# A decode step's output projection and second MLP layer: weights as the moving operand in four column strips, and the output in four transfers

## The chip, the cores and the metric

The kernel runs on one core of a Trainium2 chip. The metric is the device time of one execution in microseconds (us). The five engines run their own instruction streams and signal one another through semaphores: PE (TensorE; its weight loads are listed apart as PEld), DVE (VectorE), ACT (ScalarE), POOL (GpSimd) and SP (SyncE). SP and ACT also issue transfers (DMA).

## The reference

A decode step for 4 sequences, one token each, in bf16. An attention branch over the last 1024 positions of the caches (32 query heads, 8 key/value heads) and an MLP branch share a normalised input; the MLP's result gates the attention's.

```python
# x: (4, 1, 512); caches (4, 8, 4096, 128); wq (512, 4096); wo (4096, 512)
# w1 (512, 1792), b1 (1792); w2 (1792, 512), b2 (512)
xn = layernorm(x)
q = xn @ wq                                   # 32 heads of 128
k, v = caches[:, :, Sk - 1024:, :], each repeated for 4 heads
p = softmax(q @ k.T * 128 ** -0.5)
s = (p @ v).reshape(4, 1, 4096) @ wo          # output projection
h = gelu(layernorm(xn) @ w1 + b1)
g = silu(h @ w2 + b2)                         # second MLP layer
out = x + s * g                               # (4, 1, 512)
```

## The kernel before, in words

All input comes through SP's queue in one written-out order: `wq`, the eight key groups (one per key/value head, 1 MB each), then value group 0, `w1`, value group 1, `w2`, value groups 2 to 7, and `wo` in six pieces (three of 1 MB, then 512, 384 and 128 KB). Value group g takes the buffer of key group g and waits until that group has been transposed. ACT's queue carries the small inputs: x (L184), `b1` (L185), `b2` (L187) and, after the first norm's square root, x once more (`x16`, L251) as 16 rows of 128 for the end.

A small scheduler (`_Program`) keeps one list of operations per engine, in the order in which the program adds them. Before an operation it waits on the semaphores of those it names; every transfer has a semaphore of its own that rises by 16. Nothing is reordered: what is added first on an engine runs first there.

POOL makes the constants (identity, selection matrices, masks; also `ident32`, an identity in f32). DVE and ACT compute the two norms. PE then works through 32 tiles of keys: transpose (L278), copy by DVE (L284), scores (L297). The q projection (L362) uses four column strips: a `tile_position=(0, 32*s)` gives 32 of the array's columns to output partitions 32s to 32s+31. For each of the 8 groups, `PV` multiplies the exponentials with the values (L315) and sums the exponentials (L321), and `epilogue` divides on DVE (L328 to L333).

The MLP lies between the groups. `mlp1` (L400, L404) comes after group 0; `mlp2` and `mlp3` after group 1; `mlp4` after group 2's PV. `mlp3` first puts the bias into PSUM (L435) and then adds 14 x 4 matmuls (L442), each with a 128x128 block of `w2` as the stationary operand and 4 columns of `hT`, one per sequence, as the moving one. The result `psM[:, PS_Z:...]` has feature p of block c in partition p, column c*4+b. ACT takes the tanh (L447), and DVE makes the gate `g_sb` (L451, L453).

After the last group `to_rows` (L486, L493) collects the attention output into `OW`, 4 columns per group and quarter. `wo` then adds 128 matmuls (L507), six batches that each wait for one piece of the weight, in the same form as L442: a 128x128 block of `wo_sb` stationary, 4 columns of `OW` moving. The end is a chain: DVE multiplies with the gate (L534, 128x16), PE transposes to 16 rows of 128 (L538, in f32), DVE adds `x16` (L540), SP issues the output (L542) and waits for it.

```python
    v = add("dve", lambda e: e.tensor_tensor(
        bass.AP(sg_sb, 0, [[16, 128], [1, 4], [4, 4]]),
        psM[:, PS_W:PS_W + 16].rearrange("p (c b) -> p c b", c=4),
        g_sb[:, :].rearrange("p (c b) -> p c b", c=4), ALU.mult), t_w, mlp["g"])
    t = add("pe", lambda pe: pe.transpose(psS[0][0:16, 0:128], sg_sb[:, :], ident32[:, :]),
            v, c_id32, ex[HKV - 2])
    v = add("dve", lambda e: e.tensor_tensor(o_bf[:, :], psS[0][0:16, 0:128], x16[:, :], ALU.add),
            t, *d_x16)
    d_out = pg.dma("sp", "out", lambda e: e.dma_start(
        out.rearrange("b s (c p) -> (b s c) p", p=128), o_bf[:, :]), v)
```

Of the kernel before, what the change touches and what calls it, by code (L numbers as in the profile page):

```python
# [16 lines left out]
class _Program:  # L17
# [10 lines left out]
    def add(self, eng, fn, *deps):  # L28
        op = _Op(eng, fn, deps)
        self.ops[eng].append(op)  # L30
        return op
# [42 lines left out]
def bass_recurrent_scan__sliding_block_cached__mixer_channel_mlp__decode_kernel(  # L74
# [14 lines left out]
    ALU = mybir.AluOpType  # L89
    AF = mybir.ActivationFunctionType  # L90
    AX = mybir.AxisListType
    BF16 = dt.bfloat16
    F32 = dt.float32

    B, D = 4, 512
    HQ, HKV, DH = 32, 8, 128
# [4 lines left out]
    FC = F // 128  # L101
# [14 lines left out]
    sb = nc.alloc_sbuf_tensor  # L116
# [7 lines left out]
    w2_sb = sb([128, FC, D], BF16)  # L124
# [1 line left out]
    P_buf = sb([128, HKV, NC * 16], BF16)  # L126

    x_bf = sb([4, 512], BF16)
    x16 = sb([16, 128], BF16)

    x32 = P_buf[0:4, 4:6, :].rearrange("p g n -> p (g n)").bitcast(F32)
    xn32 = P_buf[0:4, 6:8, :].rearrange("p g n -> p (g n)").bitcast(F32)
# [12 lines left out]

    ones_bf = sb([128, 128], BF16)
    ident = sb([128, 128], BF16)
    ones32 = sb([128, 128], F32)
    ident32 = sb([128, 128], F32)
    ind = sb([128, 128], BF16)  # L150
    zero_bf = sb([128, 512], BF16)
    negm = sb([128, 512], BF16)
# [3 lines left out]
    q_sb = sb([128, 2, 512], BF16)  # L156
    qT = sb([128, 128], BF16)
    b1_sb = sb([1, F], BF16)
    b2_sb = sb([4, 128], BF16)
    sel = sb([128, 4, 32], BF16)  # L160
    OW = sb([128, 4, HKV * 4], BF16)
    hT = sb([128, 64], BF16)
# [2 lines left out]
    den_sb = sb([128, HKV * 16], F32)  # L165
    rden = sb([128, HKV * 16], F32)

    tz_sb = sb([128, 16], F32)
    sz_sb = sb([128, 16], F32)
    g_sb = sb([128, 16], F32)  # L170
    sg_sb = sb([128, 16], F32)
    o_bf = sb([16, 128], BF16)

    psK = [nc.alloc_psum_tensor("psK%d" % i, [128, 1024], BF16) for i in range(NB)]
    psS = [nc.alloc_psum_tensor("psS%d" % i, [128, 512], F32) for i in range(2)]
    psO = [nc.alloc_psum_tensor("psO%d" % i, [128, 512], F32) for i in range(2)]
    psM = nc.alloc_psum_tensor("psM", [128, 512], F32)
    PS_Z, PS_W = 192, 208

    pg = _Program(nc)  # L180
    add = pg.add
# [3 lines left out]
    d_b1 = pg.dma("act", "b1", lambda e: e.dma_start(  # L185
        b1_sb[0:1, :], B_b1.rearrange("(o n) -> o n", o=1)))
    d_b2 = pg.dma("act", "b2", lambda e: e.dma_start(  # L187
        b2_sb[:, :], B_b2.rearrange("(c n) -> c n", c=4)))

    def cache_rows(cache, g):  # L190

# [7 lines left out]
    def load_k(g):  # L199
        d_k[g] = pg.dma("sp", "k%d" % g, lambda e: e.dma_start(  # L200
            kv_buf[:, g, :, :].rearrange("p c d -> p (c d)"), cache_rows(A_k_cache, g)),
            )
# [15 lines left out]
    d_wq.append(load_wq(1))  # L218
    for g in range(2, HKV):
        load_k(g)  # L220
    x_r = A_x.rearrange("b s (c p) -> (b s c) p", p=128)


    c_1 = add("gp", lambda e: e.memset(ones_bf[:, :], 1.0))
    c_id = add("gp", lambda e: e.affine_select(
        ident[:, :], ones_bf[:, :], [[1, 128]], ALU.is_equal, 0.0,
        base=0, channel_multiplier=-1), c_1)
    c_ind = add("gp", lambda e: e.affine_select(
        ind[:, :], ones_bf[:, :], [[0, 32], [1, 4]], ALU.is_equal, 0.0,
        base=0, channel_multiplier=-1), c_1)  # L230
    c_sel = add("gp", lambda e: e.affine_select(
        sel[:, :, :], ones_bf[:, :], [[1, 4], [4, 32]], ALU.is_equal, 0.0,
        base=0, channel_multiplier=-1), c_1)
    c_xT = add("gp", lambda e: e.memset(xT[:, :, :], 0.0))
    c_yT = add("gp", lambda e: e.memset(yT[:, :, :], 0.0))
    c_z = add("gp", lambda e: e.memset(zero_bf[:, :], 0.0))
    c_neg = add("gp", lambda e: e.affine_select(
        negm[:, :], zero_bf[:, :], [[0, 32], [1, 4], [0, 4]], ALU.is_equal, NEG,
        base=0, channel_multiplier=-1), c_z)
    c_o32 = add("gp", lambda e: e.memset(ones32[:, :], 1.0))  # L240
    c_id32 = add("gp", lambda e: e.affine_select(
        ident32[:, :], ones32[:, :], [[1, 128]], ALU.is_equal, 0.0,
        base=0, channel_multiplier=-1), c_o32)


    v = add("dve", lambda e: e.tensor_copy(x32[:, :], x_bf[:, :]), d_x)  # L246
    v = add("dve", lambda e: e.bn_stats(st1[:, :], x32[:, :]), v)
    v = add("dve", lambda e: e.bn_aggr(mv1[:, :], st1[:, :]), v)
    v = add("dve", lambda e: e.tensor_single_scalar(vt1[:, :], mv1[:, 1:2], EPS, ALU.add), v)
    a = add("act", lambda e: e.activation(sq1[:, :], vt1[:, :], AF.Sqrt), v)  # L250
    d_x16 = [pg.dma("act", "x16%d" % i, lambda e, i=i: e.dma_start(  # L251
        x16[8 * i:8 * i + 8, :], x_r[8 * i:8 * i + 8, :])) for i in range(2)]
    v = add("dve", lambda e: e.reciprocal(rstd1[:, :], sq1[:, :]), a)
    v = add("dve", lambda e: e.tensor_scalar(xn32[:, :], x32[:, :], mv1[:, 0:1], rstd1[:, 0:1],
                                             op0=ALU.subtract, op1=ALU.mult), v)
    v_xn = add("dve", lambda e: e.tensor_copy(xn_bf[:, :], xn32[:, :]), v)
    v = add("dve", lambda e: e.bn_stats(st2[:, :], xn32[:, :]), v)
    v = add("dve", lambda e: e.bn_aggr(mv2[:, :], st2[:, :]), v)
    v = add("dve", lambda e: e.tensor_single_scalar(vt2[:, :], mv2[:, 1:2], EPS, ALU.add), v)
    a = add("act", lambda e: e.activation(sq2[:, :], vt2[:, :], AF.Sqrt), v)  # L260
    v = add("dve", lambda e: e.reciprocal(rstd2[:, :], sq2[:, :]), a)
# [6 lines left out]
    ex = [None] * HKV  # L268
# [118 lines left out]
    mlp = {}  # L387
# [44 lines left out]

    def mlp3():
        def fn(pe):
            last = pe.matmul(psM[:, PS_Z:PS_Z + 16], b2_sb[:, :],  # L435
                             bass.AP(ident, 0, [[128, 4], [1, 4], [0, 4]]),
                             start=True, stop=False, skip_group_check=True)
            for k in range(FC):
                s = min(k // 4, 2) if k < FC - 4 else 3
                n = (k - K0[s]) * 16 + s * 4  # L440
                for c in range(4):
                    last = pe.matmul(psM[:, PS_Z + c * 4:PS_Z + (c + 1) * 4],  # L442
                                     w2_sb[:, k, c * 128:(c + 1) * 128], hT[:, n:n + 4],
                                     start=False, stop=(k == FC - 1), skip_group_check=True)
            return last
        t = add("pe", fn, mlp["h"], d_w2, d_b2, c_id)
        mlp["tz"] = add("act", lambda e: e.activation(  # L447
            tz_sb[:, :], psM[:, PS_Z:PS_Z + 16], AF.Tanh, scale=0.5), t)

    def mlp4():  # L450
        v = add("dve", lambda e: e.tensor_scalar(sz_sb[:, :], tz_sb[:, :], 0.5, 0.5,  # L451
                                                 op0=ALU.mult, op1=ALU.add), mlp["tz"])
        mlp["g"] = add("dve", lambda e: e.tensor_tensor(  # L453
            g_sb[:, :], psM[:, PS_Z:PS_Z + 16], sz_sb[:, :], ALU.mult), v)

    NUN = HKV * NU
    for n in range(LAG, NUN + LAG):
# [7 lines left out]
    d_w2 = pg.dma("sp", "w2", lambda e: e.dma_start(  # L465
        w2_sb[:, :, :], B_w2.rearrange("(p c) o -> p c o", c=FC)))
# [30 lines left out]
    first = [True]  # L497

    def wo(k, rows):
        g0, g1, i0, i1, d = d_wo[k]  # L500

        def fn(pe):
            last = None
            for g in range(g0, g1):
                for i in range(i0, i1):
                    for c in range(4):
                        last = pe.matmul(psM[:, PS_W + c * 4:PS_W + (c + 1) * 4],  # L507
                                         wo_sb[:, g, i, c * 128:(c + 1) * 128],
                                         OW[:, i, g * 4:(g + 1) * 4],
                                         start=first[0], stop=(k == len(d_wo) - 1 and i == i1 - 1),  # L510
                                         skip_group_check=True)
                        first[0] = False
            return last
        return add("pe", fn, d, rows, mlp["g"])

    for g in range(HKV):
        PV(g)
        if g == 0:
            epilogue(0)
            mlp1()  # L520
        if g >= 2:
            epilogue(g - 1)
        if g == 1:
            mlp2()
            mlp3()
        if g == 2:
            mlp4()
    epilogue(HKV - 1)
    rows = to_rows(0, HKV)
    for k in range(len(d_wo)):  # L530
        t_w = wo(k, rows)


    v = add("dve", lambda e: e.tensor_tensor(  # L534
        bass.AP(sg_sb, 0, [[16, 128], [1, 4], [4, 4]]),
        psM[:, PS_W:PS_W + 16].rearrange("p (c b) -> p c b", c=4),
        g_sb[:, :].rearrange("p (c b) -> p c b", c=4), ALU.mult), t_w, mlp["g"])
    t = add("pe", lambda pe: pe.transpose(psS[0][0:16, 0:128], sg_sb[:, :], ident32[:, :]),  # L538
            v, c_id32, ex[HKV - 2])
    v = add("dve", lambda e: e.tensor_tensor(o_bf[:, :], psS[0][0:16, 0:128], x16[:, :], ALU.add),  # L540
            t, *d_x16)
    d_out = pg.dma("sp", "out", lambda e: e.dma_start(  # L542
        out.rearrange("b s (c p) -> (b s c) p", p=128), o_bf[:, :]), v)

    pg.plan()
    with nc.Block() as block:

        @block.gpsimd
        def _(gp):
            pg.emit("gp", gp)  # L550

        @block.vector
        def _(dve):
            pg.emit("dve", dve)

        @block.scalar
        def _(act):
            pg.emit("act", act)

        @block.sync  # L560
        def _(sp):
            pg.emit("sp", sp)
            sp.wait_ge(d_out.sem, 16)

        @block.tensor
        def _(pe):
            pg.emit("pe", pe)
# [28 lines left out]
```

The softmax here doesn't subtract the row's maximum and nothing guards it: scores larger than these inputs give would overflow.

## Time and profile before

| | |
|---|---|
| median of 12 runs | 77.04 us (76.89 to 77.14) |
| the profiled execution's own time | 77.06 us |
| its span, first to last instruction | 75.3 us |
| moved by DMA | 28.99 MB, mean 385 GB/s |
| PE busy | 51.5 us (68%), 1058 matmuls |
| DVE busy | 39.3 us (52%) |
| ACT busy | 9.8 us (13%) |
| mean granted TensorE clock | 0.826 of full speed |

How to read it: times count from the span's start. The page cuts the span into 40 slices; a digit is a busy share or a granted clock in tenths, 9 standing for 90% or more. A row of the groups gives the line, the engine, the operation, out<-in with partitions x elements, the count, then the total busy us and the mean ns of one, then the idle time just before and what ended it. In a row such as `128*32` the first number is the rows of the array that are used and the second its columns. "issue" is time in which an engine waited for nothing that the profile shows. Matmuls are pipelined: their mean length is not their spacing.

### The profile page before, as it was taken

What the parts mean: (1) busy time and instruction counts of PE and PEld (TensorE: products, weight loads), DVE (VectorE), ACT (ScalarE), POOL (GpSimd) and SP (SyncE); (2) the same over time, 40 slices, a digit from 0 to 9 for tenths busy, and PEclk for the clock granted to TensorE, in tenths of its full rate; (3) what the DMA queues carried; (4) which work ended last, traced back from release to release, by engine and by line L of the source; (5) the groups of instructions that cost most, each with busy time, mean ns of one, the idle gap of its engine ahead of it and who ended that gap; (6) DMA issues with size and microseconds to landing.
All of it is one profiled execution on the core that took longest, in us unless ns stands there. A gap on an engine that the chain in (4) does not pass through costs nothing.

```text
span 75.3 us, 2309 instructions
## 1 busy us (share of the span) xinstructions
PE 51.5 (68%) x1058; PEld 39.4 (52%) x1058; DVE 39.3 (52%) x82; ACT 9.8 (13%) x16; POOL 4.6 (6%) x14
## 2 busy tenths in 40 slices
PE   0000039974789999979959987994399999365850
PEld 0000039963269989969949911022198668164730
DVE  0878106894258989969957060004654877810010
ACT  0611000000270320303303500015000000000000
POOL 6980000000000000000000000000000000000000
PEclk9999999999999999999999996599555555555555
DMA  2899999998999999999999999999999999999600
GB/s 46 270 420 405 429 431 461 452 418 378 435 422 426 422 422 431 413 435 460 412 405 439 433 420 411 422 413 422 435 426 426 424 400 420 420 418 410 255 8 2
DMA packets 4219, 28.99 MB, mean 385 GB/s; under 512 B 493, under 2 KB 625, under 8 KB 1650
## 3 DMA queue, kind: packets, MB, share of 16 engines
q1 hardware_dynamic: 4160, 28.84, 92.1%
q8 instruction: 8, 0.13, 0.6%
q10 hardware_dynamic: 50, 0.01, 0.1%
q14 instruction: 1, 0.01, 0.0%
HBM read 28.85 MB, written 0.00 MB: 383 GB/s over the span
## 4 chain that ended last, share of the span: by engine, by line
DMA 37%; PE 34%; SPq 17%; DVE 5%; issue 4%
DMA wo_sb<-in_A_wo_dram 24%; PE psK L278 21%; SPq L475 16%; DMA kv_buf<-in_A_k_cache_dram 12%; PE psS L297 6%; DVE kt_buf L284 3%; PE psO L362 3%; PE psS L293 2%; DVE q_sb L368 1%; PE psK L374 1%; PE psM L507 1%; PE psK L346 1%; PE psS L538 1%; SPq L212 1%; SPq L205 0%
## 5 line engine op out<-in xcount | busy, mean ns | idle before, releaser
L278 PE MATMUL psK<-ident,kv_buf 128*128 128x128 bf16 x256 | 20.7, 233 | 12.2 <-DMA kv_buf<-in_A_k_cache_dram 10.7
L284 DVE COPY kt_buf<-psK 128x1024 bf16<-128x1024 bf16 x32 | 21.2, 691 | 7.9 <-PE psK L278 7.7
L278 PEld LDWEIGHTS psK<-ident,kv_buf 128*128 128x128 bf16 x256 | 16.6, 105 | 11.8 <-DMA kv_buf<-in_A_k_cache_dram 10.7
L297 PE MATMUL psS<-qT,kt_buf 128*128 128x16 bf16 x256 | 10.4, 169 | 0.2 <-issue 0.2
L297 PEld LDWEIGHTS psS<-qT,kt_buf 128*128 128x128 bf16 x256 | 9.4, 96 | 1.8 <-issue 0.9
L315 PEld LDWEIGHTS psO<-P_buf,kv_buf 128*128 128x128 bf16 x256 | 7.4, 102 | 3.0 <-issue 3.0
L315 PE MATMUL psO<-P_buf,kv_buf 128*128 128x16 bf16 x256 | 8.0, 173 | 0.2
L328 DVE TENSOR_REDUCE den_sb<-psS 128x16 f32<-128x512 f32 x8 | 5.5, 691 | 4.2 <-PE psS L321 3.9
L305 ACT ACTIVATE P_buf<-psS 128x512 bf16<-128x512 f32 x8 | 4.8, 597 | 16.5 <-PE psS L297 16.5
L507 PE MATMUL psM<-OW,wo_sb 128*128 128x4 bf16 x128 | 4.2, 166 | 2.1 <-DMA wo_sb<-in_A_wo_dram 1.0
L400 PE MATMUL psK<-w_sb,yT 128*32 128x512 bf16 x16 | 4.9, 1084 | 0.8 <-issue 0.8
L507 PEld LDWEIGHTS psM<-OW,wo_sb 128*128 128x128 bf16 x128 | 3.8, 104 | 2.5 <-issue 1.2
L321 PE MATMUL psS<-P_buf,ones_bf 128*128 128x512 bf16 x8 | 4.3, 534 | 0.0
L411 DVE SCALAR_TENSOR_TENSOR kt_buf<-kt_buf,psK 128x512 f32<-128x512 f32 x1 | 0.7, 689 | 6.1 <-ACT kt_buf L410 6.1
L534 DVE TENSOR_TENSOR sg_sb<-psM,g_sb 128x16 f32<-128x16 f32 x1 | 0.2, 185 | 5.9 <-PE psM L507 5.9
L293 PE MATMUL psS<-negm,ind 128*128 128x512 bf16 x8 | 3.0, 380 | 0.0
L400 PEld LDWEIGHTS psK<-w_sb,yT 128*32 128x32 bf16 x16 | 0.5, 114 | 3.6 <-issue 3.6
L369 ACT ACTIVATE q_sb<-psO 128x512 bf16<-128x512 f32 x1 | 0.6, 597 | 13.3 <-PE psO L362 13.3
L331 DVE RECIPROCAL rden<-den_sb 128x16 f32<-128x16 f32 x8 | 2.0, 253 | 0.3
L246 DVE CAST P_buf<-x_bf 4x512 f32<-4x512 bf16 x1 | 1.0, 953 | 2.2 <-DMA x_bf<-in_A_x_dram 2.2
L362 PE MATMUL psO<-wq_sb,xT 128*32 128x512 bf16 x32 | 1.9, 380 | 0.3 <-DVE xT L351 0.3
L424 PE MATMUL psK<-ident,kt_buf 128*128 128x128 bf16 x4 | 0.6, 305 | 2.1 <-DVE kt_buf L419 2.1
(64 smaller groups left out, 28.8 us busy)
## 6 DMA issues: line engine op xcount, KB each, us to landing
kv_buf<-in_A_k_cache_dram SPq DMA_DIRECT2D x8, 1024.0 KB, 20.6
kv_buf<-in_A_v_cache_dram SPq DMA_DIRECT2D x8, 1024.0 KB, 23.8
wq_sb<-in_A_wq_dram SPq DMA_DIRECT2D x2, 2048.0 KB, 11.4
w_sb<-in_B_w_dram SPq DMA_DIRECT2D x2, 1792.0 KB, 28.0
wo_sb<-in_A_wo_dram SPq DMA_DIRECT2D x3, 1024.0 KB, 25.0
wo_sb<-in_A_wo_dram SPq DMA_DIRECT2D x1, 512.0 KB, 21.6
wo_sb<-in_A_wo_dram SPq DMA_DIRECT2D x1, 384.0 KB, 18.3
wo_sb<-in_A_wo_dram SPq DMA_DIRECT2D x1, 128.0 KB, 18.1
```

Source lines behind the costliest of these rows:

```text
L278: last = pe.transpose(psK[n % NB][:, j * 128:(j + 1) * 128], kv_buf[:, g, u * UT + j, :], ident[:, :])
L284: cp[n] = add("dve", lambda e: e.tensor_copy(kt_buf[:, n % NKT, :], psK[n % NB][:, 0:1024]), t, sc.get(n - NKT))
L293: pe.matmul(psS[g % 2][:, 0:512], ind[:, :], negm[:, :], start=True, stop=False, skip_group_check=True)
L297: last = pe.matmul(psS[g % 2][:, c * 16:(c + 1) * 16], kt_buf[:, n % NKT, j * 128:(j + 1) * 128], qT[:, g * 16:(g + 1) * 16], start=False, ...
L305: ex[g] = add("act", lambda e: e.activation(P_buf[:, g, :], psS[g % 2][:, 0:512], AF.Exp, scale=SCALE), sc[n])
L315: last = pe.matmul(pso[:, 0:16], kv_buf[:, (HKV + g) % NS, c, :], P_buf[:, g, c * 16:(c + 1) * 16], start=(c == 0), stop=(c == NC - 1))
L321: den[g] = add("pe", lambda pe: pe.matmul(psS[g % 2][:, 0:512], ones_bf[:, :], P_buf[:, g, :], start=True, stop=True), ex[HKV - 2 + g % 2] ...
L328: v = add("dve", lambda e: e.tensor_reduce(den_sb[:, cs], bass.AP(psS[g % 2], 0, [[512, 128], [1, 16], [16, NC]]), AX.X, ALU.add), den[g])
L362: last = pe.matmul(psO[m // 4][32 * s:32 * s + 32, 0:512], xT[:, c, :], wq_sb[:, c, m * 512:(m + 1) * 512], start=(c == 0), stop=(c == 3), ...
L400: pe.matmul(psK[0][32 * s:32 * s + 32, 0:1024].bitcast(F32), yT[:, c, :], bass.AP(w1_sb, c * F + K0[s], [[4 * F, 128], [1, 4], [FC, 128]]) ...
L475: e.dma_start(wo_sb[:, g0:g1, i0:i1, :], wo_r[:, g0:g1, i0:i1, :]))))
L507: last = pe.matmul(psM[:, PS_W + c * 4:PS_W + (c + 1) * 4], wo_sb[:, g, i, c * 128:(c + 1) * 128], OW[:, i, g * 4:(g + 1) * 4], start=firs ...
```

## The change

Both operands of L442 and L507 change places. The 4 columns of `hT` or `OW` become the stationary operand, loaded into one of four column strips, and 128 columns of the weights become the moving one. Block c of the output features goes to strip c: sequence b is partition 32c+b, and its 128 features lie along the row. The first matmul of each strip loads 32 columns instead of 4, so that all 128 partitions of the PSUM area are written. The bias is added last, by four matmuls with one row of ones.

The tanh, the gate, the product and the sum now work on 128x128 instead of 128x16. The result has its features along the rows already, so the transpose, `ident32` and `ones32` go. x comes as `xs`, 4 rows into the start of each strip, by four transfers on ACT's queue that wait for a memset of `xs`; the output leaves by four transfers of 4 rows, two on SP's queue and two on ACT's. `b2` is loaded as one row. The numbers of instructions and the order on each engine are otherwise as they were.

```diff
-    x16 = sb([16, 128], BF16)
+    xs = sb([128, 128], BF16)
...
-    ones32 = sb([128, 128], F32)
-    ident32 = sb([128, 128], F32)
...
-    b2_sb = sb([4, 128], BF16)
+    b2_sb = sb([1, D], BF16)
...
-    PS_Z, PS_W = 192, 208
+    PS_Z, PS_W = 0, 128
...
-        b2_sb[:, :], B_b2.rearrange("(c n) -> c n", c=4)))
+        b2_sb[0:1, :], B_b2.rearrange("(o n) -> o n", o=1)))
...
-    x_r = A_x.rearrange("b s (c p) -> (b s c) p", p=128)
+    x_r = A_x.rearrange("b o (s p) -> s (b o) p", s=4)
+    out_r = out.rearrange("b o (s p) -> s (b o) p", s=4)
...
+    c_xs = add("gp", lambda e: e.memset(xs[:, :], 0.0))
...
-    c_o32 = add("gp", lambda e: e.memset(ones32[:, :], 1.0))
-    c_id32 = add("gp", lambda e: e.affine_select(
-        ident32[:, :], ones32[:, :], [[1, 128]], ALU.is_equal, 0.0,
-        base=0, channel_multiplier=-1), c_o32)
...
-    d_x16 = [pg.dma("act", "x16%d" % i, lambda e, i=i: e.dma_start(
-        x16[8 * i:8 * i + 8, :], x_r[8 * i:8 * i + 8, :])) for i in range(2)]
+    d_xs = [pg.dma("act", "xs%d" % s, lambda e, s=s: e.dma_start(
+        xs[32 * s:32 * s + 4, :], x_r[s]), c_xs) for s in range(4)]
...
     def mlp3():
         def fn(pe):
-            last = pe.matmul(psM[:, PS_Z:PS_Z + 16], b2_sb[:, :],
-                             bass.AP(ident, 0, [[128, 4], [1, 4], [0, 4]]),
-                             start=True, stop=False, skip_group_check=True)
+            last = None
             for k in range(FC):
...
+                m = 32 if k == 0 else 4
                 for c in range(4):
-                    last = pe.matmul(psM[:, PS_Z + c * 4:PS_Z + (c + 1) * 4],
-                                     w2_sb[:, k, c * 128:(c + 1) * 128], hT[:, n:n + 4],
-                                     start=False, stop=(k == FC - 1), skip_group_check=True)
+                    pe.matmul(psM[32 * c:32 * c + m, PS_Z:PS_Z + 128], hT[:, n:n + m],
+                              w2_sb[:, k, c * 128:(c + 1) * 128],
+                              start=(k == 0), stop=False, tile_position=(0, 32 * c))
+            for c in range(4):
+                last = pe.matmul(psM[32 * c:32 * c + 4, PS_Z:PS_Z + 128], ones_bf[0:1, 0:4],
+                                 b2_sb[0:1, c * 128:(c + 1) * 128],
+                                 start=False, stop=True, tile_position=(0, 32 * c))
             return last
-        t = add("pe", fn, mlp["h"], d_w2, d_b2, c_id)
+        t = add("pe", fn, mlp["h"], d_w2, d_b2)
...
                     for c in range(4):
-                        last = pe.matmul(psM[:, PS_W + c * 4:PS_W + (c + 1) * 4],
+                        m = 32 if first[0] else 4
+                        last = pe.matmul(psM[32 * c:32 * c + m, PS_W:PS_W + 128],
+                                         OW[:, i, g * 4:g * 4 + m],
                                          wo_sb[:, g, i, c * 128:(c + 1) * 128],
-                                         OW[:, i, g * 4:(g + 1) * 4],
                                          start=first[0], stop=(k == len(d_wo) - 1 and i == i1 - 1),
-                                         skip_group_check=True)
-                        first[0] = False
+                                         tile_position=(0, 32 * c))
+                    first[0] = False
...
     v = add("dve", lambda e: e.tensor_tensor(
-        bass.AP(sg_sb, 0, [[16, 128], [1, 4], [4, 4]]),
-        psM[:, PS_W:PS_W + 16].rearrange("p (c b) -> p c b", c=4),
-        g_sb[:, :].rearrange("p (c b) -> p c b", c=4), ALU.mult), t_w, mlp["g"])
-    t = add("pe", lambda pe: pe.transpose(psS[0][0:16, 0:128], sg_sb[:, :], ident32[:, :]),
-            v, c_id32, ex[HKV - 2])
-    v = add("dve", lambda e: e.tensor_tensor(o_bf[:, :], psS[0][0:16, 0:128], x16[:, :], ALU.add),
-            t, *d_x16)
-    d_out = pg.dma("sp", "out", lambda e: e.dma_start(
-        out.rearrange("b s (c p) -> (b s c) p", p=128), o_bf[:, :]), v)
+        sg_sb[:, :], psM[:, PS_W:PS_W + 128], g_sb[:, :], ALU.mult), t_w, mlp["g"])
+    v = add("dve", lambda e: e.tensor_tensor(o_bf[:, :], sg_sb[:, :], xs[:, :], ALU.add),
+            v, c_xs, *d_xs)
+    d_out = [pg.dma("act" if s % 2 else "sp", "out%d" % s, lambda e, s=s: e.dma_start(
+        out_r[s], o_bf[32 * s:32 * s + 4, :]), v) for s in range(4)]
...
-            sp.wait_ge(d_out.sem, 16)
+            for d in d_out:
+                sp.wait_ge(d.sem, 16)
```

More of the change, by code (lines that the diff above doesn't have):

```diff
@@ L166, in bass_recurrent_scan__sliding_block_cached__mixer_channel_mlp__decode_kernel @@
     rden = sb([128, HKV * 16], F32)
[L168 to L172, printed above, removed]
+    tz_sb = sb([128, 128], F32)
+    g_sb = sb([128, 128], F32)
+    sg_sb = sb([128, 128], F32)
+    o_bf = sb([128, 128], BF16)
     psK = [nc.alloc_psum_tensor("psK%d" % i, [128, 1024], BF16) for i in range(NB)]
@@ L440, in fn @@
                 n = (k - K0[s]) * 16 + s * 4
+                m = 32 if k == 0 else 4
                 for c in range(4):
-                    last = pe.matmul(psM[:, PS_Z + c * 4:PS_Z + (c + 1) * 4],
-                                     w2_sb[:, k, c * 128:(c + 1) * 128], hT[:, n:n + 4],
-                                     start=False, stop=(k == FC - 1), skip_group_check=True)
+                    pe.matmul(psM[32 * c:32 * c + m, PS_Z:PS_Z + 128], hT[:, n:n + m],
[5 more added lines that the diff above has]
+                                 start=False, stop=True, tile_position=(0, 32 * c))
             return last
-        t = add("pe", fn, mlp["h"], d_w2, d_b2, c_id)
+        t = add("pe", fn, mlp["h"], d_w2, d_b2)
         mlp["tz"] = add("act", lambda e: e.activation(
-            tz_sb[:, :], psM[:, PS_Z:PS_Z + 16], AF.Tanh, scale=0.5), t)
+            tz_sb[:, :], psM[:, PS_Z:PS_Z + 128], AF.Tanh, scale=0.5), t)
     def mlp4():
-        v = add("dve", lambda e: e.tensor_scalar(sz_sb[:, :], tz_sb[:, :], 0.5, 0.5,
+        v = add("dve", lambda e: e.tensor_scalar(tz_sb[:, :], tz_sb[:, :], 0.5, 0.5,
                                                  op0=ALU.mult, op1=ALU.add), mlp["tz"])
         mlp["g"] = add("dve", lambda e: e.tensor_tensor(
-            g_sb[:, :], psM[:, PS_Z:PS_Z + 16], sz_sb[:, :], ALU.mult), v)
+            g_sb[:, :], psM[:, PS_Z:PS_Z + 128], tz_sb[:, :], ALU.mult), v)
     NUN = HKV * NU
```

## The prediction

> **What bounds the kernel now.** I read the page's slices first, then the chain of work that ended last, then the timeline of its last 6 us, then the groups with shapes kept apart for prices.
>
> From the page's 40 slices (1.88 us each): the TensorE clock granted, and the busy tenths of the DMA engines.
>
> ```profile
> PEclk9999999999999999999999996599555555555555
> DMA  2899999998999999999999999999999999999600
> ```
>
> Counted from 0, the transfers are saturated from slice 2 to slice 36 (to 69.7 us), so the weights and caches coming in set the time, and all arithmetic that keeps up with them is free. From slice 28 on the clock is half of full speed: all that the change touches runs there. The chain in order of time (start, us, what) shows the exposed end:
>
> ```profile
> 53.64 18.29 DMA wo_sb<-in_A_wo_dram
> 71.93 0.05 issue
> 71.98 0.60 PE psM L507 x16
> ...
> 72.60 0.20 DVE sg_sb L534
> ...
> 72.84 0.40 PE psS L538
> ...
> 73.26 0.28 DVE o_bf L540
> ```
>
> The last rows of `wo` land at 71.93. Then come the 16 matmuls that need them, the product with the gate, the transpose, the addition of x, and the output's transfer. The change can win or lose time only in these 3.4 us, unless it makes TensorE fall behind the transfers. The timeline of TensorE shows how far that is (in brackets its idle time before, and who ended it):
>
> ```profile
> 69.80 1.01 PE L507 MATMUL psM<-OW,wo_sb 128*128 128x4 bf16 x32 [0.38 <-DMA wo_sb<-in_A_wo_dram]
> 71.02 0.58 PE L507 MATMUL psM<-OW,wo_sb 128*128 128x4 bf16 x16 [0.20 <-DMA wo_sb<-in_A_wo_dram]
> 71.98 0.58 PE L507 MATMUL psM<-OW,wo_sb 128*128 128x4 bf16 x16 [0.38 <-DMA wo_sb<-in_A_wo_dram]
> ```
>
> TensorE waits for data three times, 0.38 + 0.20 + 0.38 = 0.96 us: so much may be lost ahead of 71.93 before the end moves.
>
> **Edit 1: the projection through strips (L507).** The count stays 128. Before, a weight tile of 128x128 is loaded and 4 columns stream; after, 4 columns of `OW` are loaded into one of four strips and 128 columns of `wo` stream. These groups give the price of both:
>
> ```profile
> L507 PE MATMUL psM<-OW,wo_sb 128*128 128x4 bf16 x128 | 4.2, 166 | 2.1 <-DMA wo_sb<-in_A_wo_dram 1.0 <-issue 0.6 <-DVE OW L493 0.5
> L362 PE MATMUL psO<-wq_sb,xT 128*32 128x512 bf16 x32 | 1.9, 380 | 0.3 <-DVE xT L351 0.3
> L486 PE MATMUL psS<-OTb,sel 128*32 128x32 bf16 x16 | 0.3, 193 | 1.3 <-DVE OTb L333 1.3
> L453 DVE TENSOR_TENSOR g_sb<-psM,sz_sb 128x16 f32<-128x16 f32 x1 | 0.2, 176 | 0.0
> L419 DVE TENSOR_TENSOR kt_buf<-kt_buf,psK 128x512 bf16<-128x512 f32 x1 | 0.7, 690 | 0.0
> ```
>
> Before: 32 matmuls take 1.01 us, of which 0.166 is the last one's own length, so they start (1.01 - 0.166)/31 = 0.027 us apart. The kernel already uses four strips in L362: its 32 matmuls of 512 columns take 1.91 us in one stretch, at full clock. That is 8 rounds of four; (1.91 - 0.38)/7 = 0.218 us a round. Four strips therefore run at once, and the loads do not show. For 128 columns at half clock a round is 0.218/4 x 2 = 0.109 us, or 0.027 us a matmul: the same pace as before. The upper end comes from L486, four rounds of 32 columns at half clock: (0.30 - 0.193)/3 = 0.036 us a round, 0.144 if all of it grows with the columns. I take 0.109, since L362 has the same long streams. The last matmul is longer: 166 ns at 4 columns and 193 at 32 give 0.96 ns a column, hence 0.285 us at 128 (L424, 128 columns at half clock, has 0.305). The last 16 matmuls are 4 rounds: 3 x 0.109 + 0.285 = 0.61 us against 0.58, **+0.03** (up to 3 x 0.144 + 0.305 = 0.74, +0.16; not below 0 at this clock).
>
> The Trainium skill, page "TensorE: Matmul & The Clock Gate", Part 3, "The mechanism", says that a weight load overlaps running matmuls only when its row group differs; all strips here have one row group, so by that rule each round would show a load, 0.10 us more for each of them, and the sum below would be a clear loss. L362 speaks against it: 0.218 us a round leaves nothing for a load beside 512 columns.
>
> **Edit 2: the second MLP layer (L435, L442).** Before 54.71 to 56.48. After: 14 rounds and one of the bias, from 54.71 on, at 0.109; the next PV's weights load from 54.71 + 15 x 0.109 = 56.35, before 56.32. At 0.144 it is 0.55 us later; that would pass through PV and `to_rows` to L507 and be met by the 0.96 us of waits. The tanh at L447 (184 ns for 16 columns) becomes some 0.28, the two DVE steps behind it 175 + 176 become some 0.23 + 0.29; all three together end 0.27 us later, and DVE has 0.70 us free before the next sum (L328 at 57.82), which is what would be late next. **0**, 0.3 if that cover is gone.
>
> **Edit 3: the transpose goes.** Before, from the chain: 72.60 to 73.54, 0.94 us (0.20 DVE, 0.40 TensorE, 0.28 DVE, and the gaps). After: a product of 128x128 from PSUM and a sum of 128x128 from SBUF. The product: 176 ns at 16 columns and 690 at 512 give 1.04 ns a column, 0.29 us. The sum's inputs are in SBUF: at most L540's 0.278 (as long, but from PSUM), at least the 0.175 that L451 takes for 16 columns from SBUF; I take 0.23, and 0.04 between the two. 0.56 us: **-0.38** (-0.30 to -0.44). The four waits on `xs` and one on GpSimd that stand before the sum are passed while the product runs, on signals given 60 us earlier, as L540's two were at 72.61 in the trace.
>
> **Edit 4: four transfers for the output.** Before: one issue on SP, and SP's wait. The issues in the timeline of both queues, and SP's wait from the list of waits (total, times, longest):
>
> ```profile
> 0.80 0.54 ACTq L184 DMA_DIRECT2D x_bf<-in_A_x_dram  x1
> 1.38 0.23 ACTq L185 DMA_DIRECT2D b_sb<-in_B_b_dram  x1
> 1.63 0.26 ACTq L187 DMA_DIRECT2D b_sb<-in_B_b_dram  x1
> 4.31 0.76 ACTq L251 DMA_DIRECT2D x<-in_A_x_dram  x2
> 73.56 0.36 SPq L542 DMA_DIRECT2D out_dram<-o_bf  x1
> ```
>
> ```profile
> SPq L546 <- DMA out_dram<-o_bf: 1.0, 1, 1.0
> ```
>
> The output has 16 rows of 256 B: 0.36 us of issue, 1.04 more to landing (1.40 in the page's list of issues). After, SP and ACT issue two each, side by side, of 4 rows of 256 B. `b2` before has exactly that shape: 0.26. Others: 0.23 (one row), 0.38 (`x16`, 8 rows), 0.54 (`x_bf`, 4 rows, the very first on its queue). I take 0.26. From the end of an issue to use of the data it is 1.04 for the output and 0.88 for the 4 rows of `x_bf` (issue over at 1.34, L246 starts on them at 2.22); I take 0.96. The second one of each queue lands at 0.26 + 0.03 + 0.26 + 0.96 = 1.51 against 1.40: **+0.11** (with 0.23 and 0.88, -0.03; with 0.38 and 0.96, +0.35; with 0.54, +0.67). SP then has four signals to pass instead of one; a DVE wait instruction on two signals takes 0.05 in the trace, so **+0.04**. What stands behind ACT's new wait for the sum: nothing, its last work is L447 at 56.5.
>
> The skill, page "DMA: Bandwidth & Descriptors", "Rules for kernel authors", tells to coalesce small transfers, since under 64 KB one mostly pays overhead, and it adds that a second queue saves only issue time. Paying the whole 1.40 us twice on each queue would make it +1.4; the trace shows no two small stores in a row, but L185 and L187 issue 0.25 us apart, so I do not take it.
>
> **Edits at the start.** `xs` comes by four issues where `x16` had two: at 0.38 each 4.31 + 1.52 = 5.83, and ACT's next work (L260) starts at 6.79; its new wait for the memset is met, as that ends near 2.6. GpSimd gains a memset (0.20) and loses one with a select (0.56). `b2` is one row instead of four. SP's queue of loads is not moved. **0**; if the issues cost over 0.62 each the norms of the MLP branch would start late, and 10.7 us, when TensorE starts, covers them still.
>
> **Sum.** +0.03 - 0.38 + 0.11 + 0.04 = -0.20 us on the profiled execution's 77.06 (span 75.3 and 1.76 around it): 76.86. The median was 77.04, 0.02 under it: **76.84**. All low ends together give -0.43, 76.6; its likely range is 76.65 to 77.05.
>
> **Rivals.**
> *Issue at `x16`'s price, 0.38:* the output's term is +0.35 and the sum +0.04: 77.08, no change. For it: `x16` has 256 B rows too and was issued in steady work. [...]
> *Slower, by the output's queues:* an issue costs what `x_bf`'s cost, 0.54, because ACT has issued nothing for 65 us, or four transfers hold one another up. +0.67 in place of +0.11: +0.36, 77.40. It decides from 0.36 an issue on (break-even) and is measurable from 0.44. Against: SP's own issue after 14 us of rest cost 0.36 for 16 rows, with all of its fixed part.
> *Slower, by strips that do not overlap with their loads:* a load in L486 has 0.106, so 0.21 us a round: from 66.84 on 16 rounds and the 0.60 stall end at 70.8, 16 more at 74.1, then 0.08 of the last one's length: 1.6 us late, 78.4 or more. Against: L362 and L486.
> *The clock comes back:* four streaming strips look busier than 4 columns. At full clock the last 16 take 3 x 0.055 + 0.22 (L374) = 0.38 in place of 0.61: 76.61. Against: from 55 to 64 us TensorE was over 90% busy in every slice of the page and stayed at half clock.
>
> **Numbers.** Forecast 0.58, of it 0.42 under -0.2% and 0.16 within 0.2%. About 0.2% (0.15 us) is what a measurement of this kernel can tell from no change. `x16`'s price 0.14 (0.12 same, 0.02 slower), the queues 0.15, no overlap 0.06, the clock 0.07 (faster). That is 0.49 faster, 0.28 same, 0.23 slower. The range from 76.60 to 77.35 leaves out the lack of overlap (0.06), the dear half of the queues (0.08) and a little below.
>
> **What would show it.** The stretch from the last `wo` landing to the end of L507's matmuls: 0.65 us at most if the strips overlap. From there to the sum's end 0.6 us. Each output issue near 0.26, and the last landing some 1.5 us after the first issue; 1.75 or more means the queues took the gain. If TensorE no longer waits for `wo` before its last 16 matmuls, edit 1 is wrong. If `wo` lands over 0.3 us away from 71.93, something moved that I hold untouched.

## The result, and the profile after

The changed kernel takes 77.22 us (median of 11 runs, 77.05 to 77.36), the kernel before 76.97 us (47 runs, the 12 that were known ahead of the prediction among them; 76.84 to 77.14). The ratio is 1.0028, with a 95% interval from 1.0020 to 1.0037: slower by 0.2 us, where 0.2 us faster was forecast. The profiled execution took 77.23 us, with a span of 75.4.

The end of the chain of the changed kernel in order of time (start, us, what):

```profile
53.74 18.08 DMA wo_sb<-in_A_wo_dram
71.82 0.04 issue
71.86 0.63 PE psM L507 x9
72.49 0.02 issue
72.52 0.30 DVE sg_sb L534
72.82 0.02 issue
72.84 0.29 DVE o_bf L536
```

The landing of weights that the chain shows, the last piece but one of `wo`, comes at 71.82 (71.93 before); the last piece, by its semaphore in the trace, comes at 72.15 (72.23 before). So nothing ahead of the end was lost. The sum is done at 73.13, where it was 73.54: the transpose's time is gone, as forecast. And yet the span is 0.1 us longer; all of the loss lies behind the chain's last line. The timeline of the two queues and the list of SP's waits:

```profile
73.16 0.66 SPq L538 DMA_DIRECT2D out_dram<-o_bf  x2
73.17 0.62 ACTq L538 DMA_DIRECT2D out_dram<-o_bf  x2
```

```profile
SPq L560 <- DMA out_dram<-o_bf: 1.1, 1, 1.1
```

One issue of 0.36 us has become two of 0.66 together, and SP's wait behind them has not become shorter. TensorE's timeline and, from the groups by shape, the new steps:

```profile
69.68 1.02 PE L507 MATMUL psM<-wo_sb,OW 128*4 128x128 bf16 x32 [0.17 <-DMA wo_sb<-in_A_wo_dram]
70.92 0.60 PE L507 MATMUL psM<-wo_sb,OW 128*4 128x128 bf16 x16 [0.22 <-DMA wo_sb<-in_A_wo_dram]
71.86 0.61 PE L507 MATMUL psM<-wo_sb,OW 128*4 128x128 bf16 x16 [0.35 <-DMA wo_sb<-in_A_wo_dram]
```

```profile
L507 PE MATMUL psM<-wo_sb,OW 128*4 128x128 bf16 x124 | 4.3, 305 | 1.4 <-DMA wo_sb<-in_A_wo_dram 0.7 <-issue 0.7
L534 DVE TENSOR_TENSOR sg_sb<-psM,g_sb 128x128 f32<-128x128 f32 x1 | 0.3, 293 | 6.0 <-PE psM L507 6.0
L536 DVE TENSOR_TENSOR o_bf<-sg_sb,xs 128x128 bf16<-128x128 f32 x1 | 0.3, 292 | 0.0
```

32 matmuls take 1.02 us after 1.01 before, and TensorE still waits for data ahead of all three batches (0.17, 0.22, 0.35): the strips keep their pace, with their loads hidden.

For the rest I divide the end of each profiled execution into five stretches at six events of the trace, so that executions can be compared whatever came earlier: the landing of the last piece of `wo`, the start of the product (L534), the first output issue, the last landing of the output, the start of SP's last own instruction, the end of the span. A landing is the last rise of the transfer's semaphore in the trace's records. Times in us; "measured" is the ratio to before less 1, times 77.0.

| kernel | `wo` to product | product to issue | issue to landing | landing to SP's end | to the span's end | sum | sum less before | measured |
|---|---|---|---|---|---|---|---|---|
| before | 0.37 | 0.97 | 1.37 | 0.18 | 0.22 | 3.10 | | |
| changed | 0.37 | 0.65 | 1.72 | 0.32 | 0.22 | 3.27 | +0.17 | +0.22 |
| one transfer | 0.32 | 0.64 | 1.18 | 0.18 | 0.22 | 2.55 | -0.55 | -0.53 |
| one signal | 0.38 | 0.65 | 1.72 | 0.18 | 0.22 | 3.15 | +0.04 | +0.02 |
| before, four transfers | 0.35 | 0.97 | 1.72 | 0.32 | 0.22 | 3.57 | +0.47 | +0.52 |
| all four on SP | 0.37 | 0.65 | 2.21 | 0.25 | 0.22 | 3.69 | +0.59 | +0.57 |
| one on each queue | 0.40 | 0.65 | 1.36 | 0.18 | 0.22 | 2.80 | -0.30 | -0.27 |
| moved, three engines | 0.37 | 1.09 | 1.27 | 0.18 | 0.22 | 3.13 | +0.03 | +0.06 |
| moved, two engines | 0.37 | 1.08 | 1.28 | 0.18 | 0.22 | 3.12 | +0.02 | 0.00 |
| moved, bf16 | 0.40 | 1.01 | 1.26 | 0.18 | 0.22 | 3.07 | -0.04 | -0.04 |
| before, bf16 transpose | 0.35 | 0.80 | 1.35 | 0.18 | 0.22 | 2.90 | -0.20 | -0.16 |
| one signal, bf16 | 0.38 | 0.58 | 1.74 | 0.18 | 0.22 | 3.10 | 0.00 | +0.06 |

The last two columns agree within 0.06 us: what these kernels differ by is their end.

### The profile page after: what moved, and what is told of

Its sections match the earlier page's. It is cut to its first block, busy times and chain, and to the rows that moved or that the text cites. A ratio compares the mean times of both kernels' runs of the same rounds, so it can differ in the third digit from the quotient of the medians.

```text
span 75.4 us, 2320 instructions
## 1 busy us (share of the span) xinstructions
PE 51.5 (68%) x1060; PEld 38.3 (51%) x1060; DVE 39.3 (52%) x82; ACT 9.8 (13%) x16; POOL 4.2 (6%) x13
## 4 chain that ended last, share of the span: by engine, by line
DMA 36%; PE 33%; SPq 18%; DVE 6%; issue 4%
DMA wo_sb<-in_A_wo_dram 24%; PE psK L274 20%; SPq L474 17%; DMA kv_buf<-in_A_k_cache_dram 12%; PE psS L293 6%; DVE kt_buf L280 4%; PE psO L358 3%; PE psS L289 2%; DVE q_sb L364 1%; PE psM L507 1%; PE psK L370 1%; PE psK L342 1%; SPq L209 1%; SPq L202 0%; DVE sg_sb L534 0%
## 5 line engine op out<-in xcount | busy, mean ns | idle before, releaser
L507 PE MATMUL psM<-wo_sb,OW 128*4 128x128 bf16 (+1 forms) x128 | 4.4, 304 | 1.9 <-DMA wo_sb<-in_A_wo_dram 0.7
L507 PEld LDWEIGHTS psM<-wo_sb,OW 128*4 128x4 bf16 (+1 forms) x128 | 2.9, 113 | 3.3 <-DMA wo_sb<-in_A_wo_dram 1.6
L534 DVE TENSOR_TENSOR sg_sb<-psM,g_sb 128x128 f32<-128x128 f32 x1 | 0.3, 293 | 6.0 <-PE psM L507 6.0
```

The lines of the kernel that those rows point to most:

```text
L507: last = pe.matmul(psM[32 * c:32 * c + m, PS_W:PS_W + 128], OW[:, i, g * 4:g * 4 + m], wo_sb[:, g, i, c * 128:(c + 1) * 128], start=first[ ...
```

## The experiments

Theory A: the four output transfers and their four signals took the gain. Theory B, the rival: they cost what was forecast, and the loss lies elsewhere (the loads at the start, the strips, the stream of weights).

**One transfer instead of four.** `for s in range(4)` of `d_out` becomes `range(1)`.

> Leaves out three of the four output transfers (and SP's waits for them); three quarters of the output are not written. Theory A, the output's four transfers and four signals took the gain: from the end of the sum to the end of the span the changed kernel takes 0.49 us more than the kernel before, so without three of them it is 77.22 - 0.49 = 76.73 us, 0.24 us faster than before. Theory B, the four transfers cost what was predicted (0.15 us) and the loss lies elsewhere (four small loads at the start, the strips, the stream of weights): 77.07 us.

Measured: 76.51 us, ratio 0.9931 (0.9909 to 0.9953). The trace's timeline:

```profile
72.47 0.29 DVE L534 TENSOR_TENSOR sg_sb<-psM,g_sb 128x128 f32<-128x128 f32 x1 [4.54 <-PE psM L507]
72.79 0.29 DVE L536 TENSOR_TENSOR o_bf<-sg_sb,xs 128x128 bf16<-128x128 f32 x1
73.11 0.35 SPq L538 DMA_DIRECT2D out_dram<-o_bf  x1
```

B's 77.07 us is excluded and A holds in kind, but the gain is twice A's figure: 0.53 us faster than before, where A said 0.24. The change's arithmetic end is worth half a microsecond as long as one issue carries the output, and the three further transfers cost 0.7 us. Two details tell where the rest of the gain comes from. The issue of 4 rows takes 0.35 us, hardly less than that of 16 rows (0.36); but from its end to landing it is 0.83 instead of 1.01. And in this execution the granted clock returned for the last stretch (the windows; us from the start, then us, and busy time of the engines, granted clock, DMA):

```profile
67.86:71.27 3.41, 2.53 (x90) 2.27 (x94) 0.07 (x1) 0.00 (x0) 0.00 (x0) 0.50 0.86 341
71.27:74.60 3.33, 1.09 (x50) 0.59 (x38) 0.58 (x2) 0.00 (x0) 0.00 (x0) 1.00 0.08 24
```

It shortened the way from the weights to the product by 0.05 us only (0.32 against 0.37; 0.35 to 0.40 in the other rows of the table), since in both kernels the last four matmuls start some 0.04 us after the landing of the last piece.

**One signal.** One semaphore for the four transfers, and one wait.

```diff
+    for d in d_out:
+        d.sem = d_out[0].sem
...
-            for d in d_out:
-                sp.wait_ge(d.sem, 16)
+            sp.wait_ge(d_out[0].sem, 64)
```

> The four output transfers share one semaphore and SP waits once, for 64. In the trace of the changed kernel SP needs 0.32 us from the last landing to its last own instruction, in that of before 0.18. Theory A: 0.13 us less than the changed kernel, 77.09 us. Theory B, a wait costs the 0.04 us predicted for all: 77.18 us.

Measured: 77.09 us, ratio 1.0003 (0.9992 to 1.0013), 0.0025 under the changed kernel's. A again: from the last landing to SP's last instruction it is 0.18 us as in the kernel before, against 0.32 with four signals. Issue and landing stay at 1.72.

**The four transfers alone, on the kernel before.**

```diff
-    d_out = pg.dma("sp", "out", lambda e: e.dma_start(
-        out.rearrange("b s (c p) -> (b s c) p", p=128), o_bf[:, :]), v)
+    out_r = out.rearrange("b s (c p) -> (b s c) p", p=128)
+    d_out = [pg.dma("act" if s % 2 else "sp", "out%d" % s, lambda e, s=s: e.dma_start(
+        out_r[4 * s:4 * s + 4, :], o_bf[4 * s:4 * s + 4, :]), v) for s in range(4)]
```

> The kernel before, with its output alone in four transfers of four rows, two on SP's queue and two on ACT's, with four semaphores, as in the change. Theory A: 76.97 + 0.49 = 77.46 us. Theory B: 76.97 + 0.15 = 77.12 us.

Measured: 77.60 us, ratio 1.0067 (1.0049 to 1.0086), +0.52 us where A said 0.49. The timeline has the changed kernel's two issues behind the old sum:

```profile
73.36 0.28 DVE L540 TENSOR_TENSOR o_bf<-psS,x 16x128 bf16<-16x128 f32 x1 [0.47 <-PE psS L538]
73.67 0.66 SPq L543 DMA_DIRECT2D out_dram<-o_bf  x2
73.67 0.62 ACTq L543 DMA_DIRECT2D out_dram<-o_bf  x2
```

The part does alone what it does in the change, so the loss does not come from how the strips lay the rows out.

**All four on SP's queue.** `"act" if s % 2 else "sp"` becomes `"sp"`.

> The changed kernel with all four output transfers on SP's queue. If an issue costs 0.34 us whatever the other queue does (0.30 and a gap of 0.04), the fourth starts at 1.1 us instead of the second at 0.39, and the end is 0.7 us later: 77.9 us. If an issue was lengthened by the other queue's issuing at the same moment and costs 0.26 alone, as predicted, the fourth ends 0.26 x 4 + 0.03 x 3 = 1.13 us after the first begins, 0.47 us later than now: 77.7 us.

Measured: 77.64 us, ratio 1.0074 (1.0057 to 1.0092), 0.35 us over the changed kernel, less than either figure. The timeline:

```profile
73.28 1.33 SPq L538 DMA_DIRECT2D out_dram<-o_bf  x4
```

Singly the issues take 0.34, 0.27, 0.30 and 0.30 us. The first is as long as beside ACT's (0.34), so the other queue does not lengthen it, and 0.26 was too low for a first issue. But each of the four lands 0.83 to 0.88 us after its issue's end; SP's two in the changed kernel needed 1.01 and 1.06, ACT's two 0.89 and 0.92. That difference was in neither figure and is asked for next.

**One transfer on each queue.** `range(4)` becomes `range(2)`.

> The changed kernel with two output transfers, one on SP and one on ACT; half of the output is not written. It asks for the second part of the loss: from the end of SP's issue to its landing it was 1.01 and 1.06 us in the changed kernel, 0.83 to 0.88 where SP's queue alone carried the output (the kernels with one transfer and with all on SP). If the two queues delay one another, SP's landing takes 1.0 us here too and the kernel is 0.2 us slower than with one transfer, ratio to before 0.9955. If it is the number of transfers in flight that delays, SP's landing takes 0.83 to 0.88 and the ratio is 0.9935 to 0.994.

Measured: 76.68 us, ratio 0.9965 (0.9950 to 0.9979). The timeline:

```profile
73.26 0.34 SPq L538 DMA_DIRECT2D out_dram<-o_bf  x1
73.27 0.27 ACTq L538 DMA_DIRECT2D out_dram<-o_bf  x1
```

SP's transfer lands 1.02 us after its issue's end, ACT's 0.90. So it is the transfer from the second queue beside it, not the number in flight: four on SP's queue alone land after 0.83 to 0.88 us. The second queue saves serial issues, and it delays SP's landing by some 0.18 us. Which part of the hardware the queues share there, no run here shows.

**Moved strips: fewer transfers by copies.** The sum goes into a wider tile, three strips are copied down to partitions 0 to 3, and one transfer of four rows of 1 KB takes all.

```diff
+    v = add("dve", lambda e: e.tensor_tensor(o4[:, 0:128], sg_sb[:, :], xs[:, :], ALU.add),
+            v, c_xs, *d_xs)
+    mv = [v]
+    for c, eng in ((1, "dve"), (2, "act"), (3, "gp")):     # two engines: (3, "dve")
+        src, dst = o4[32 * c:32 * c + 4, 0:128], o4[0:4, c * 128:(c + 1) * 128]
...
+    d_out = [pg.dma("sp", "out", lambda e: e.dma_start(
+        out.rearrange("b o d -> (b o) d"), o4[0:4, :]), *mv)]
```

> The changed kernel, but the sum goes into the first 128 columns of a tile of 512, strips 1, 2 and 3 are then copied into partitions 0 to 3 by DVE, ACT and GpSimd, one each and side by side, and one transfer of four rows of 1 KB takes the whole output. If the four transfers are all that the change lost by, the copies cost what their longest costs: a hop of 0.04 and some 0.22 us of ACT (L446 has 0.28 for 128 columns from PSUM), so 0.26 us after the one-transfer kernel, 0.27 us faster than before: ratio 0.9965. Rival, short steps over three engines are as dear as transfers (GpSimd 0.4 us or more for its copy): no faster than before, ratio 1.000.

> The same with strips 1 and 3 copied by DVE and strip 2 by ACT, none by GpSimd. If the four transfers are all that the change lost by: DVE 0.04 + 2 x 0.16 = 0.36 us after the one-transfer kernel, 0.17 us faster than before, ratio 0.998. Rival: ratio 1.000 or more.

> The same as with two engines, and the product of projection and gate is kept in bf16 instead of f32, so that both inputs of the sum have two bytes. If the sum's 0.29 us is a matter of its f32 input, it falls to some 0.2 us: 0.26 us faster than before, ratio 0.9965. Rival, its length is one column per cycle whatever the type: as with two engines.

Measured: ratio 1.0008 (0.9999 to 1.0018) with three engines, 1.0000 (0.9989 to 1.0012) with two, 0.9995 (0.9986 to 1.0005) with two and the product in bf16 (`sg_sb` in BF16). With the product in f32 the rival was right: not faster than before. The third stays far from the 0.9965 that was expected, too, and is not told from two engines. The timeline of the last:

```profile
72.81 0.23 DVE L536 TENSOR_TENSOR o<-sg_sb,xs 128x128 bf16<-128x128 bf16 x1
73.07 0.31 ACT L542 ACTIVATE o<-o 4x128 bf16<-4x128 bf16 x1 [17.29 <-DVE o L536]
73.07 0.40 DVE L544 COPY o<-o 4x128 bf16<-4x128 bf16 x2
73.50 0.33 SPq L545 DMA_DIRECT2D out_dram<-o  x1
```

ACT's copy of 4x128 takes 0.31 us (I had 0.22), DVE's 0.18 each, GpSimd's 0.31 (the rival had 0.4 or more); with the hops the issue comes 0.43 us later than straight behind the sum. Rows of 1 KB land 0.93 us after the issue, against 0.83 for 256 B. With bf16 on both inputs the sum falls from 0.29 to 0.23; that much of the third expectation came true.

**Sixteen rows by one transfer.** `OW` and `hT` get another order of columns, so that a window of 25 columns brings the four sequences to columns 0, 8, 16 and 24 of a strip, and the 16 result rows to partitions 0, 8, ... 120.

```diff
+            bass.AP(OW, 0, [[128, 128], [32, 4], [1, 8], [8, 4]]),
...
-                        m = 32 if first[0] else 4
+                        m = 32 if first[0] else 25
...
-                                         OW[:, i, g * 4:g * 4 + m],
+                                         OW[:, i, g:g + m],
...
+    d_out = [pg.dma("sp", "out", lambda e: e.dma_start(out_r, rows16(o_bf)), v)]
```

> The changed kernel with another order of the columns of OW and hT, so that a stationary window of 25 columns has the four sequences in its columns 0, 8, 16 and 24 (other columns between them). The 16 rows of the result then lie in partitions 0, 8, 16, ... 120, one constant step, and one transfer takes them all, by one issue on SP; xs comes by one load in the same way. If four transfers were all that the change lost by, the end is that of the one-transfer kernel (0.35 us of issue, 0.83 to landing) or, with 16 rows in flight, that of before (1.01 to landing): ratio to before 0.993 to 0.9955, 76.4 to 76.65 us. Rival, loads of 25 columns no longer hide behind four streams of 128: each round of four is 0.1 us longer, TensorE falls behind the weights, ratio 1.01 or more.

> The same with the product of projection and gate kept in bf16. The sum took 0.225 us instead of 0.292 with it in the kernel with moved strips: 0.07 us less than with sixteen rows alone, ratio lower by 0.0009. Rival, another engine or SP's wake-up hides it: the same ratio as with sixteen rows alone.

Measured: 1.0019 (1.0007 to 1.0031), and 1.0006 (0.9993 to 1.0019) with bf16. The first met neither of its two figures; the second is lower by 0.0013 where 0.0009 was expected, but the intervals overlap, so its rival is not excluded. The timeline of the first:

```profile
68.19 0.71 DVE L495 CAST OW<-psS 128x128 bf16<-128x128 f32 x1 [0.42 <-PE psS L488]
...
69.05 4.00 PE L510 MATMUL psM<-wo_sb,OW 128*32 128x128 bf16 x128 [0.93 <-DVE OW L495]
...
73.73 0.70 SPq L541 DMA_DIRECT2D out_dram<-o_bf  x1
```

Loads of 25 columns hide as well: 128 matmuls in 4.00 us, 0.031 each with a pause of 0.4 us among them. But the one issue takes 0.70 us, as much as two, and lands 1.05 us later: the transfers were saved by number, not by time. Two things set it apart from the 16 rows of the kernel before (0.36 us): its destination is 4 blocks of 4 rows, and its source rows lie 8 partitions apart. Which of them costs the time, no run separates. And `OW`'s copy with its scattered columns takes 0.71 us instead of 0.29. This profiled execution (77.59 us) is far above its kernel's median (77.16): TensorE began on `wo` 2.4 us later than in the changed kernel's profile and no longer waited for weights, so its end is not put into the table. Of these 2.4 us 1.7 are there at the bias of the first MLP layer already (50.67 us against 48.99), ahead of the new column orders; 0.4 are `OW`'s copy. The execution with bf16 was of the same kind (77.46 us, median 77.05). Of 12 executions each, three of the first took 77.3 us or more (77.59, 77.58, 77.34) and one of the second; what makes them late is open. With the changed kernel's 0.37 us from `wo` to the product the end of the first would be 3.16 us by an estimate from its other stretches, +0.06 on before, and measured is +0.15.

**Both ends trimmed.** The kernel before with its product and its transpose in bf16; and the changed kernel with one signal and its product in bf16.

```diff
-    sg_sb = sb([128, 16], F32)
+    sg_sb = sb([128, 16], BF16)
...
-    t = add("pe", lambda pe: pe.transpose(psS[0][0:16, 0:128], sg_sb[:, :], ident32[:, :]),
-            v, c_id32, ex[HKV - 2])
-    v = add("dve", lambda e: e.tensor_tensor(o_bf[:, :], psS[0][0:16, 0:128], x16[:, :], ALU.add),
+    t = add("pe", lambda pe: pe.transpose(psK[2][0:16, 0:128], sg_sb[:, :], ident[:, :]),
+            v, c_id)
+    v = add("dve", lambda e: e.tensor_tensor(o_bf[:, :], psK[2][0:16, 0:128], x16[:, :], ALU.add),
```

> The kernel before, with its product of projection and gate in bf16 and the transpose in bf16 too (identity and PSUM area that exist already). It asks how much of what the change removes lay in the transpose's f32 rather than in the transpose. L538 takes 0.383 us in f32, L424 0.305 for 128 columns in bf16 at the same clock; the sum, which took 0.278 with an f32 input from PSUM, takes 0.225 to 0.278: 0.08 to 0.13 us less, ratio 0.9983 to 0.999, 76.85 to 76.95 us. Rival, a matmul's time from its start to the next engine's start is set by the clock and the columns alone: ratio 1.000.

> The changed kernel with one semaphore for its four output transfers and the product in bf16: both terms of the changed end that can be trimmed while the four transfers stay. From the kernel with one signal (ratio 1.0003) less 0.067 us: ratio 0.9994, no faster than before by more than 0.1%. If the two gains do not add, 1.0003.

Measured: 76.84 us for the first, ratio 0.9979 (0.9969 to 0.9988), faster than both kernels; 77.03 us and 1.0008 (0.9993 to 1.0022) for the second, not told from before and compatible with both of its figures. The timeline of the first:

```profile
72.56 0.19 DVE L534 TENSOR_TENSOR sg_sb<-psM,g_sb 128x16 bf16<-128x16 f32 x1 [6.88 <-PE psM L507]
72.81 0.28 PE L538 MATMUL psK<-ident,sg_sb 128*16 128x128 bf16 x1 [0.29 <-DVE sg_sb L534]
73.12 0.21 DVE L540 TENSOR_TENSOR o_bf<-psK,x 16x128 bf16<-16x128 bf16 x1 [0.37 <-PE psK L538]
73.36 0.36 SPq L542 DMA_DIRECT2D out_dram<-o_bf  x1
```

The transpose falls from 0.38 to 0.28 and the sum from 0.28 to 0.21: from product to issue 0.80 us instead of 0.97. Half of what the change gains there (0.32 us) is to be had with the transpose kept, and without one more transfer.

## Why the prediction was wrong, point by point

The mechanism was right and three terms of the sum were mis-sized, one of them by more than the whole forecast gain. From the table, changed less before:

| term | forecast | measured |
|---|---|---|
| last matmuls (edit 1) | +0.03 | 0.00 |
| product, transpose, sum (edit 3) | -0.38 | -0.32 |
| issue to landing (edit 4) | +0.11 | +0.35 |
| four signals (edit 4) | +0.04 | +0.14 |
| sum | -0.20 | +0.17 |

*Edit 4, issue to landing, is the step that failed.* It was 0.26 + 0.03 + 0.26 + 0.96. Measured on SP: 0.34 + 0.04 + 0.28 + 1.06. Of the 0.21 us between them 0.11 are issue and 0.10 landing (0.03 more come from before's own 1.37, which I had read as 1.40). For the issue I had taken `b2`'s row because it had the same shape. But `b2` was the third issue in a row on its queue, and in the runs here the first on SP is the longer one: 0.34 for the first, 0.27 to 0.30 for those behind it. The row to take was SP's own 0.36 for 16 rows; the issue hardly depends on the rows. For the landing I had taken the middle between 16 rows and 4 rows, as if only rows counted; the run with one transfer on each queue shows that the second queue counts, by 0.18 us. The text named both prices as ends (0.38 an issue; "four transfers hold one another up") and gave them 0.14 and 0.15 of the chance. 0.36 an issue was stated as the point where the gain is gone, and SP's issue of 16 rows at exactly 0.36 was argued away as having a fixed part: it is nearly all fixed. The sign that was set for lost gain, a last landing 1.75 us after the first issue, was a little too high: it came at 1.72, and the gain was gone.

*The four signals* cost 0.14 us, since SP passes its waits one after another and the transfer that lands last stands first among them: behind its landing come two further wait steps, of 0.06 and 0.07 us. With one signal for all they are gone (0.18). The DVE instruction that I took for a price stood beside other work.

*Edit 3* gave 0.32 instead of 0.38: the sum of 128x128 with one f32 input takes 0.292 us, as long as the product from PSUM. I had taken 0.23 for it, as if SBUF made it quicker; 0.23 is right for two bf16 inputs.

*Edit 1* was right in pace (0.027 us a matmul) and the exposed loads never came. The sentence that the prediction took from the Trainium skill, page "TensorE: Matmul & The Clock Gate", Part 3, "The mechanism", that a weight load overlaps running matmuls only when its row group differs, does not hold for these column strips: 32 matmuls with 32 loads take 1.02 us. The +0.03 is 0.00 in the table only because the table counts from another landing. The prediction took 71.93 for the landing of the last rows of `wo`; it is that of the last piece but one, and the last comes at 72.23. Counted from the landing that it took, the product starts after 0.67 us in the kernel before and after 0.70 in the changed one, the +0.03 of the forecast; counted from the last landing it is 0.37 in both. After the change the last four matmuls wait for the last piece (they start at 72.19, it lands at 72.15); before they did not (72.29, 72.23).

*Edit 2* was right in its effect and not in its size: from the first matmul of L437 to the next PV's load it takes 56.04 - 54.22 = 1.82 us, against 1.61 before and 1.64 forecast; the weight loads stand still for 0.22 of it, ahead of the four bias matmuls (one row). The cover of 0.96 us was there, and 0.74 of it are left.

*The start* was right: the four `xs` issues take 1.37 us, and ACT's next work begins at 6.85 where it began at 6.79.

*The clock rival* needs the correction above: in the one execution that had it, full clock at the end was worth some 0.05 us, not 0.23.

*The rule to coalesce*, from the Trainium skill, page "DMA: Bandwidth & Descriptors", section "Rules for kernel authors", was weighed and its price not taken. Its direction was the right one: three more transfers cost 0.7 us. Its other half holds too, with a remark: against all four on SP the second queue saved 0.67 us of issue (0.66 against 1.33), of which the kernel kept 0.35, since it delayed SP's landing by some 0.18 us and added a wait step.

## What to carry to other kernels

At a kernel's exposed end, count issues and signals before bytes or rows: here an output issue costs some 0.3 us whether it carries 4 rows or 16 in one step (one in a 4 x 4 pattern cost 0.70), the rows moved the landing by at most 0.18 us, and further signals can add steps of 0.06 to 0.07 us behind the last landing. A layout that saves a transpose has to be followed to its last transfer: 0.3 us of arithmetic were bought with 0.5 us of transfers. Before a step is removed, see what it costs in its cheaper form, in bf16 here.

## What the runs showed that I had not expected

- A transfer of 4 rows of 256 B on SP's queue lands 0.83 us after its issue's end, one of 16 rows 1.01, one of 4 rows of 1 KB 0.93; beside a transfer from ACT's queue the first takes 1.02.
- One issue with a destination of 4 blocks of 4 rows, from source rows 8 partitions apart, takes 0.70 us, against 0.36 for 16 rows in one step on both sides.
- Copies of 4x128 take 0.31 us on ACT and on GpSimd, 0.18 on DVE.
- Four column strips with stationary windows of 4 and of 25 columns stream at the same pace, 0.027 us a matmul at half clock while nothing else holds them up.
